# A decode layer on one core: TensorE's program as a loop of four turns, K and V loaded head by head, the maximum gathered by TensorE, w1 loaded behind wq

## The chip, the core and the metric

One core of a Trainium2 chip runs the kernel. The metric is device time in microseconds (us) of one execution; the kernel before takes 111.0 us (median of 3 runs, 110.99 to 111.12). Its engines: TensorE (PE; PEld is its weight load), VectorE (DVE), ScalarE (ACT), GpSimd (POOL), and SyncE (SP), whose queue issues the large loads. 16 DMA engines carry all loads.

## The reference

```python
xn = layernorm(x)                                          # x: 2 x 1 x 448
q  = xn @ wq                                               # 16 heads of 256
k, v = the last 2048 positions of the caches, 8 heads, each used by 2 heads of q
s  = softmax(q k / 16) v @ wo                              # 4096 -> 448
g  = silu(relu(xn @ w1) @ w2)                              # 448 -> 1792 -> 448
return x + s * g
```

All inputs are bf16. Of the 44 MB that are read, K and V are 33.5 MB (2 batches x 8 heads x 2048 x 256, twice), wq and wo 3.67 MB each, w1 and w2 1.61 MB each.

## The kernel before, in words

**Units.** The attention is done in four units `u`: one batch and four of the eight K/V heads, 4 MiB of K and 4 MiB of V each. A unit's position is split into 32 blocks `kb` of 64 positions `t`. `load_k` and `load_v` (lines 279, 282) move a unit with one DMA each; `unit_src` (line 197) puts block kb of head h on partition 4 kb + h, so that the four heads are interleaved over all 128 partitions, one row of 32 KiB on each.

**A unit's steps.** `do_T` (line 312): DVE transposes 32x32 blocks of K (pairs of bf16 as one fp32) from `kbuf` to `kt`, in four pieces. `do_S` (line 318): 32 matmuls in four column groups of TensorE make the scores, 8 rows in each quarter of the partitions; the moving operand takes every eighth bf16 of `kt` (step of 16 bytes). `ch_max` (line 330): DVE takes each row's maximum and shares it over the heads' rows by two 32x32 transposes and a second maximum; ACT's exponential follows. `ch_spread` (line 344): 16 matmuls lay the exponentials out by position, and one more sums them. `ch_pt` (line 355): DVE copies this with a mask. `do_PV` (line 363): 32 matmuls, in four column groups, with contiguous rows of V. `do_o_pe`, `do_at_exp`, `do_at` (lines 375 to 401): the unit's output is turned and scaled into `at2`.

**The second branch.** `do_h`, `do_hn`, `do_hT`, `do_hs` (lines 408 to 433) and `do_F` (line 450) are the two layers with w1 and w2.

**The end.** `at2` meets wo's 32 row groups j (lines 531 to 544). wo comes in five DMAs (`WO_PARTS`). The first 24 groups run in four column groups (`tiled`, line 435), each 448 columns wide, whose partial sums `fold_sums` (line 440) copies and adds; the last 8 groups run as four narrow matmuls each, straight into the result.

**What sets the order.** Each engine runs its instructions in the order in which lines 202 to 551 append them to `_Prog.lists`; a wait on a semaphore is put before an instruction that needs another engine's result. The order is written out by hand: unit u+1's scores stand between unit u's steps, with two buffers each for K, `kt`, the scores, the exponentials and `pt`. SP's order is wq, K0, K1, V0, K2, K3, V1, V2, w1, V3, w2, and wo's five parts. V2 goes to a K buffer (`vhome`, line 211), w1 and w2 to `kt[0]` after unit 2's scores.

Of the kernel before, what the change touches and what calls it, by code (L numbers as in the profile page):

```python
# [5 lines left out]
BF = mybir.dt.bfloat16  # L6
# [9 lines left out]
class _Op:  # L16
    __slots__ = ("eng", "fn", "deps", "dma", "needed", "value", "sem")

    def __init__(self, eng, fn, deps, dma):
        self.eng, self.fn, self.deps, self.dma = eng, fn, deps, dma  # L20
        self.needed, self.value, self.sem = dma, 0, None


class _Prog:


    def __init__(self, nc, es):
        self.nc, self.es = nc, es
        self.lists = {PE: [], DVE: [], ACTE: [], SP: [], POOL: []}

    def op(self, eng, fn, deps=()):
        o = _Op(eng, fn, [d for d in deps if d is not None], False)
        self.lists[eng].append(o)
        return o

    def dma(self, eng, dst, src, deps=()):
        o = _Op(eng, lambda e: e.dma_start(dst, src), [d for d in deps if d is not None], True)
        self.lists[eng].append(o)
        return o

    def run(self):
# [3 lines left out]
        for ops in self.lists.values():  # L45
            for o in ops:
                for d in o.deps:
                    d.needed = True
        for e, ops in self.lists.items():
            sem, count = self.es.enter_context(self.nc.semaphore(f"s_{e}")), 0  # L50
            for o in ops:
                if o.dma:
                    n += 1
                    o.sem, o.value = self.es.enter_context(self.nc.semaphore(f"d_{n}")), 16
                elif o.needed:
                    count += 1
                    o.sem, o.value = sem, count
        engines = ((POOL, nc.gpsimd), (SP, nc.sync), (ACTE, nc.scalar), (PE, nc.tensor), (DVE, nc.vector))
        for name, eng in engines:
            hint = eng.mark_branch_hint_location() if name == DVE else None  # L60
            self.emit(eng, self.lists[name])
            if hint is not None:
                eng.br("fin").branch_hint(hint)
        nc.switch_bb("fin")

    def emit(self, eng, ops):
        seen = {}
        for o in ops:
# [9 lines left out]
            if o.needed:  # L78
                made.then_inc(o.sem, 16 if o.dma else 1)


def bass_recurrent_scan__sliding_block_cached__dense_activation_relu__decode_kernel(
# [30 lines left out]
    WO_PARTS = [10, 10, 4, 6, 2]  # L113
    WO_TILED = 24

    es = contextlib.ExitStack()
    with es:
# [21 lines left out]
        hmask = named("hmask", [128, 4], F32)  # L139
# [9 lines left out]
        q_big = named("q_big", [128, NU * NG * 32], BF)  # L149
# [7 lines left out]
        mx = named("mx", [128, 32], F32)  # L157
        mxt = named("mxt", [128, 32], F32)
        nbt = named("nbt", [128, 32], F32)
        nb = [named(f"nb{i}", [128, 32], F32) for i in range(2)]  # L160
        ssum = [named(f"ssum{i}", [128, 1], F32) for i in range(2)]
        rs = [named(f"rs{i}", [128, 1], F32) for i in range(NU)]
        e_sb = [named(f"e_sb{i}", [128, 512], BF) for i in range(2)]
        pt = [named(f"pt{i}", [128, 512], BF) for i in range(2)]
        fs = named("fs", [128, D], F32)
        o_sb = named("o_sb", [128, 512], BF)
        at_exp = named("at_exp", [128, 64], BF)
# [3 lines left out]
        kt = [named(f"kt{i}", [128, UW], BF) for i in range(2)]  # L171
        wq_sb = kt[1]
        wo_sb = kbuf[1]
        w1_sb = kt[0]
        W2_AT = SLOTS * FC

        sp = psum("sp", [128, 2048], F32)
        sbk = [sp[:, 512 * i:512 * i + 512] for i in range(2)]
# [18 lines left out]
        def unit_src(u, cache):  # L197
            hf, b = divmod(u, 2)
            return cache[b, HU * hf:HU * hf + HU, SK - W:SK, :].rearrange("h (kb t) d -> kb h (t d)", t=TS)
# [11 lines left out]
        vhome = [vbuf, vbuf, kbuf[0], vbuf]  # L211
        d_k, d_v = {}, {}
# [7 lines left out]
        p_qb = pr.op(POOL, lambda e: e.memset(q_big[:, :].bitcast(F32), 0.0))  # L220
        p_s0 = pr.op(POOL, lambda e: e.memset(sel[:, :].bitcast(F32), 0.0))
        p_mx = pr.op(POOL, lambda e: e.memset(mx[:, :], 0.0))
        p_nbt = pr.op(POOL, lambda e: e.memset(nbt[:, :], 0.0))
# [3 lines left out]
        a_z = [pr.op(ACTE, lambda e, t=t: e.memzero(t[:, :])) for t in (mbk, gbk, hbk)]  # L227
# [21 lines left out]
        def fold_op(e):  # L249
# [3 lines left out]
        v_hm = pr.op(DVE, lambda e: e.tensor_reduce(  # L253
            out=hmask[:, :], in_=view(ident, 0, [[1, 4], [4, 32]]), axis=AX.X, op=ALU.add), [p_id])

        def fold8_op(e):
            with nc.allow_low_precision("zeros and ones"):
                return e.tensor_reduce(out=fold8[:, :], in_=view(ident, 0, [[32, 4], [4, 2], [1, 4]]), axis=AX.X, op=ALU.add)
        v_f8 = pr.op(DVE, fold8_op, [p_id])
        v_ss = pr.op(DVE, lambda e: e.tensor_copy(  # L260
            view(sumsel, 0, [[64, 2], [8, 8], [1, 8]]), view(fold8, 0, [[0, 2], [1, 8], [0, 8]])), [v_f8])
        v_ff = pr.op(DVE, lambda e: e.tensor_copy(fold_f[:, :], fold[:, 0:17]), [v_fold])
        for r in range(2):
            v_sel = pr.op(DVE, lambda e, r=r: e.tensor_copy(
                view(sel, 1024 * r, [[132, 8], [32, 4], [1, 4]]), view(ident, 4 * r, [[0, 8], [1, 4], [32, 4]])), [p_s0, p_id])
# [7 lines left out]
        for r in range(1, 4):  # L273
            v_xr = pr.op(DVE, lambda e, r=r: e.tensor_copy(
                view(xr, 32 * r, [[128, SLOTS], [1, 4]]), view(xr, 0, [[128, SLOTS], [1, 4]])), [v_xr])
# [3 lines left out]
        def load_k(u, deps=()):  # L279
            d_k[u] = pr.dma(SP, kbuf[u % 2][:, :], unit_src(u, A_k_cache), deps)  # L280

        def load_v(u, deps=()):
            d_v[u] = pr.dma(SP, vhome[u][:, :], unit_src(u, A_v_cache), deps)


        def do_q():
# [19 lines left out]
            for qd in range(4):  # L306
                st["q"] = pr.op(DVE, lambda e, qd=qd: e.tensor_copy(  # L307
                    view(q_big, qd, [[NG * 32, NU], [32, NG], [4, 8]], n=32, p0=32 * qd),
                    view(q_t, 0, [[1, NU], [32, NG], [256, 8]], n=32, p0=32 * qd)), [v, p_qb])


        def do_T(u, c):
            src, dst = kbuf[u % 2][:, :].bitcast(F32), kt[u % 2][:, :].bitcast(F32)
            deps = [d_k[u], st.get(("S", u - 2))] + ([st["q_mm"]] if u == 1 else [])
            st["T", u] = pr.op(DVE, lambda e: e.transpose(  # L315
                dst[:, 2048 * c:2048 * c + 2048], src[:, 2048 * c:2048 * c + 2048]), deps)

        def do_S(u):
            deps = [st["T", u], st["q"], st.get(("exp", u - 2)), *st["q_n"]]
            for gp in range(NG):  # L320
                for h in range(HU):
                    lo = (u * NG + gp) * 32 + 8 * h
                    o = pr.op(PE, mm(sbk[u % 2][32 * h:32 * h + 8, :], q_big[:, lo:lo + 8],
                                     view(kt[u % 2], 64 * (gp // 2) + gp % 2 + 2 * h, [[256, TS], [8, 8]]),
                                     gp == 0, gp == NG - 1, tile_position=(0, 32 * h)), deps)
                    deps = []
            st["S", u] = o


        def ch_max(u):  # L330
            k = u % 2
            v = pr.op(DVE, lambda e: e.tensor_reduce(out=mx[:, 0:1], in_=sbk[k], axis=AX.X, op=ALU.max),  # L332
                      [st["S", u], p_mx, st.get("mxt")])
            v = st["mxt"] = pr.op(DVE, lambda e: e.transpose(mxt[:, :], mx[:, :]), [v, st.get("neg")])  # L334
            v = st["neg"] = pr.op(DVE, lambda e: e.tensor_reduce(
                out=view(nbt, 0, [[4, 2], [1, 4]]), in_=view(mxt, 0, [[4, 2], [0, 4], [1, 4]]),
# [244 lines left out]
```

## Time and profile before

| | |
|---|---|
| median of 3 runs | 111.0 us |
| the profiled execution | 111.33 us |
| its span, first to last instruction | 109.9 us |
| moved by the DMA engines | 44.16 MB, mean 402 GB/s |
| PE, DVE, ACT busy | 68.5, 59.8, 12.2 us |
| instructions | 1131 (490 matmuls, 469 weight loads) |

The profiled execution is 0.33 us over the median, and 1.4 us of it lie outside the span. Busy time is a mean over stages with different limits; a matmul's length is modelled, and matmuls in different column groups overlap, so the time from the first to the last of a group says more than the sum of their lengths.

### The profile page before, as it was taken

The page shows a single profiled execution, that of the slowest core. Times are in us where ns is not written, and L with a number is a line of the kernel's source. Part 1 is how long each engine was busy: PE and PEld are TensorE (multiplying, and loading weights), DVE is VectorE, ACT ScalarE, POOL GpSimd, SP SyncE. Part 2 cuts the span into 40 slices and gives each one's busy share as a digit, 9 for nine tenths or more (in the row PEclk, how much of TensorE's full clock was granted, in tenths as well). Part 3 has the DMA queues.
Part 4 walks back from the last instruction along what each step waited for, and adds up shares of the span by engine and source line. Part 5 has one row for each costly group of instructions (what it writes and reads, how often), then busy time and mean ns, then how long its engine had stood idle before and what let it go on. Part 6 is the DMA issues. An engine that isn't in the chain of part 4 may idle for free.

```text
span 109.9 us, 1131 instructions
## 1 busy us (share of the span) xinstructions
PE 68.5 (62%) x490; PEld 23.3 (21%) x469; DVE 59.8 (54%) x84; ACT 12.2 (11%) x21; POOL 4.4 (4%) x14
## 2 busy tenths in 40 slices
PE   0010699500001995579995699989999892556871
PEld 0000001000000110553110622146213841211330
DVE  2167000399999996825984879995005026003621
ACT  2930000340000000201000200040001300020000
POOL 7800000000000000000000000000000000000000
PEclk9999999995555599656999755999999999955555
DMA  6798998999899989989999999999899998999920
GB/s 168 334 460 388 513 430 382 418 489 430 382 501 441 394 382 525 430 382 406 483 430 394 430 489 406 394 477 447 344 425 496 453 406 363 413 433 417 413 115 1
DMA packets 2463, 44.16 MB, mean 402 GB/s; under 512 B 282, under 2 KB 412, under 8 KB 924
## 3 DMA queue, kind: packets, MB, share of 16 engines
q1 hardware_dynamic: 2432, 44.11, 94.3%
q8 instruction: 3, 0.05, 0.2%
q10 hardware_dynamic: 28, 0.01, 0.0%
HBM read 44.11 MB, written 0.00 MB: 402 GB/s over the span
## 4 chain that ended last, share of the span: by engine, by line
DMA 36%; PE 32%; DVE 26%; issue 2%; ACT 1%; SPq 0%
DMA kbuf<-in_A_wo_dram 26%; PE sp L187 23%; DVE kt L315 15%; DMA kt<-in_A_wq_dram 10%; PE sp L192 6%; DVE q_t L305 2%; DVE mx L332 2%; DVE q_big L307 2%; PE gbk L187 2%; ACT e_sb L339 1%; PE hbk L187 1%; DVE q_n L299 1%; DVE pt L356 1%; DVE mxt L334 1%; DVE nb L338 1%
## 5 line engine op out<-in xcount | busy, mean ns | idle before, releaser
L187 PE MATMUL sp<-kt,q_big 128*8 128x512 bf16 x128 | 30.1, 1088 | 14.4 <-DVE kt L315 14.4
L315 DVE STREAM_TRANSPOSE kt<-kbuf 128x2048 f32<-128x2048 f32 x16 | 35.6, 2274 | 2.8 <-DMA kbuf<-in_A_k_cache_dram 2.7
L187 PEld LDWEIGHTS sp<-kt,q_big 128*8 128x8 bf16 x128 | 4.7, 103 | 34.0 <-issue 18.4
L187 PE MATMUL sp<-e_sb,sel 128*128 128x64 bf16 x64 | 8.1, 294 | 5.3 <-ACT e_sb L339 5.3
L187 PE MATMUL sp<-vbuf,pt 128*16 128x512 bf16 x96 | 8.0, 492 | 2.4 <-DMA vbuf<-in_A_v_cache_dram 1.9
L187 PEld LDWEIGHTS sp<-e_sb,sel 128*128 128x128 bf16 x64 | 7.0, 119 | 8.2 <-ACT e_sb L339 8.2
L339 ACT ACTIVATE e_sb<-sp,nb 128x512 bf16<-128x512 f32 x4 | 2.8, 688 | 51.5 <-DVE nb L338 51.5
L332 DVE TENSOR_REDUCE mx<-sp 128x1 f32<-128x512 f32 x4 | 2.7, 687 | 9.4 <-PE sp L187 9.4
L192 PE MATMUL sp<-kt,xr 128*128 128x512 bf16 x21 | 7.7, 488 | 0.0
L299 DVE TENSOR_SCALAR q_n<-sp 128x1024 bf16<-128x1024 f32 x1 | 1.2, 1225 | 10.5 <-PE sp L192 10.5
L187 PE MATMUL sp<-kt,xr 128*128 128x512 bf16 x7 | 3.6, 512 | 3.7 <-DMA kt<-in_A_wq_dram 3.7
L187 PE MATMUL mbk<-ident,xg 2*128 2x2 bf16 x7 | 0.3, 163 | 7.9 <-DVE xg L237 7.9
L356 DVE TENSOR_TENSOR pt<-sp,hmask 128x512 bf16<-128x512 f32 x4 | 2.8, 698 | 4.2 <-PE sp L187 4.2
L387 DVE TENSOR_TENSOR at_exp<-mbk,qmask 128x64 bf16<-128x64 f32 x4 | 0.8, 204 | 7.2 <-PE mbk L187 7.2
L187 PEld LDWEIGHTS sp<-vbuf,pt 128*16 128x16 bf16 x96 | 3.1, 120 | 7.0 <-DMA vbuf<-in_A_v_cache_dram 3.7
L372 ACT ACTIVATE o_sb<-sp 128x512 bf16<-128x512 f32 x4 | 2.4, 593 | 17.9 <-PE sp L187 17.9
L399 DVE TENSOR_SCALAR at<-mbk,rs 64x32 bf16<-64x32 f32 x4 | 1.4, 350 | 3.6 <-PE mbk L187 3.6
L187 PEld LDWEIGHTS sp<-kt,xr 128*128 128x128 bf16 x7 | 0.8, 121 | 10.7 <-issue 6.9
L187 PE MATMUL gbk<-kbuf,at 128*17 128x448 bf16 x24 | 3.0, 570 | 0.1
L302 ACT ACTIVATE q_n<-sp 128x1024 bf16<-128x1024 f32 x1 | 1.0, 1024 | 14.5 <-PE sp L192 14.5
L187 PE MATMUL gbk<-kt,h_sb 128*17 128x448 bf16 x14 | 1.7, 569 | 1.3 <-DMA kt<-in_B_w_dram 1.3
L305 DVE STREAM_TRANSPOSE q_t<-q_n 128x2048 bf16<-128x2048 bf16 x1 | 2.3, 2311 | 0.0
(74 smaller groups left out, 45.8 us busy)
## 6 DMA issues: line engine op xcount, KB each, us to landing
kbuf<-in_A_k_cache_dram SPq DMA_DIRECT2D x4, 4096.0 KB, 17.9
vbuf<-in_A_v_cache_dram SPq DMA_DIRECT2D x3, 4096.0 KB, 21.6
kbuf<-in_A_v_cache_dram SPq DMA_DIRECT2D x1, 4096.0 KB, 18.7
kt<-in_A_wq_dram SPq DMA_DIRECT2D x1, 3584.0 KB, 11.2
kt<-in_B_w_dram SPq DMA_DIRECT2D x2, 1568.0 KB, 19.3
kbuf<-in_A_wo_dram SPq DMA_DIRECT2D x2, 1120.0 KB, 27.3
kbuf<-in_A_wo_dram SPq DMA_DIRECT2D x1, 672.0 KB, 29.3
kbuf<-in_A_wo_dram SPq DMA_DIRECT2D x1, 448.0 KB, 29.1
```

What stands on the lines that cost most here:

```text
L187: return lambda e: e.matmul(out_ap, lhsT=lhsT, rhs=rhs, start=start, stop=stop, skip_group_check=True, **kw)
L192: return lambda e: e.add_instruction(mybir.InstMatmult(name=nc.get_next_instruction_name(), start_tensor_calc=start, stop_tensor_calc=stop ...
L299: e.tensor_scalar(out=view(q_n, 0, [[64, 16], [32, 2], [1, 32]]), in0=view(sp, 0, [[64, 16], [1, 2], [2, 32]]), scalar1=SCALE, scalar2=Non ...
L305: v = pr.op(DVE, lambda e: e.transpose(q_t[:, :], q_n[:, :]), halves)
L307: st["q"] = pr.op(DVE, lambda e, qd=qd: e.tensor_copy(view(q_big, qd, [[NG * 32, NU], [32, NG], [4, 8]], n=32, p0=32 * qd), view(q_t, 0, [ ...
L315: st["T", u] = pr.op(DVE, lambda e: e.transpose(dst[:, 2048 * c:2048 * c + 2048], src[:, 2048 * c:2048 * c + 2048]), deps)
L332: v = pr.op(DVE, lambda e: e.tensor_reduce(out=mx[:, 0:1], in_=sbk[k], axis=AX.X, op=ALU.max), [st["S", u], p_mx, st.get("mxt")])
L334: v = st["mxt"] = pr.op(DVE, lambda e: e.transpose(mxt[:, :], mx[:, :]), [v, st.get("neg")])
L339: st["exp", u] = pr.op(ACTE, lambda e: e.activation(e_sb[k][:, :], sbk[k], ACT.Exp, bias=nb[k][:, 0:1], accum_out=ssum[k][:, 0:1]), [v, st ...
L356: st["pt", u] = pr.op(DVE, lambda e: e.tensor_tensor(out=view(pt[u % 2], 0, [[128, 4], [1, 128]]), in0=view(sp, 1024, [[0, 4], [1, 128]]), ...
L372: st["osb", u] = pr.op(ACTE, lambda e: e.activation(o_sb[:, :], obk[:, :], ACT.Copy), [o, st.get(("oT", u - 1))])
L399: st["at", u] = st["mbk"] = pr.op(DVE, lambda e: e.tensor_scalar(out=view(at2, 16 * b, [[32, 32]], n=64, p0=p0), in0=mbk[p0:p0 + 64, 32:64 ...
```

## The change

- **TensorE's program is a loop.** After wq's and w1's matmuls, a loop `pe_loop` of four turns does one unit a turn, one step after the other, with waits against a register that counts the turns. A block for w2 is entered in the fourth turn alone. `kt`, the scores, the exponentials, `pt` and V have one buffer each.
- **K and V.** A load moves one head: head h goes to partitions 32 h to 32 h + 31, one row of 32 KiB on each. A unit's K takes four DMAs instead of one, and so does its V; V of units 2 and 3 comes in halves of positions, eight DMAs, the first half as soon as the first 16 matmuls of the unit before have read it.
- **Scores.** With this layout a column group of TensorE takes eight blocks kb of all four heads, and the moving operand takes every second bf16 (step of 4 bytes). A unit's q is laid out by four small ACT copies in each turn instead of by DVE once.
- **Maximum.** A multiply on DVE and a matmul with a matrix of zeros and ones replace the two transposes.
- **w1** is loaded to V's buffer right behind wq, and its layer is done ahead of the loop, on ACT instead of DVE. w2 goes to the buffer that held wq.
- **wo** comes in parts of 10, 12, 6, 2, 2 groups instead of 10, 10, 4, 6, 2, and 28 groups instead of 24 run in column groups.
- SP's order is wq, w1, K0, K1, V0, K2, V1, K3, V2 (halves), w2, V3 (halves), wo.

The diff, cut to its core:

```diff
-    WO_PARTS = [10, 10, 4, 6, 2]
-    WO_TILED = 24
+    WO_PARTS = [10, 12, 6, 2, 2]
+    WO_TILED = 28
...
-        def unit_src(u, cache):
+        def cache_src(u, cache, h):
             hf, b = divmod(u, 2)
-            return cache[b, HU * hf:HU * hf + HU, SK - W:SK, :].rearrange("h (kb t) d -> kb h (t d)", t=TS)
+            return cache[b, HU * hf + h, SK - W:SK, :].rearrange("(kb t) d -> kb (t d)", t=TS)
...
         def load_k(u, deps=()):
-            d_k[u] = pr.dma(SP, kbuf[u % 2][:, :], unit_src(u, A_k_cache), deps)
+            d_k[u] = [pr.dma(SP, kbuf[u % 2][32 * h:32 * h + 32, :], cache_src(u, A_k_cache, h), deps) for h in range(HU)]
...
+        def load_v_half(u, k):
+            lo, hi = k * UW // 2, (k + 1) * UW // 2
+            for h in range(HU):
+                pr.dma(SP, vbuf[32 * h:32 * h + 32, lo:hi], cache_src(u, A_v_cache, h)[:, lo:hi],
+                       [st["PV" if k else "PVa", u - 1]], kind="VB" if k else "VA")
...
         def ch_max(u):
-            v = st["mxt"] = pr.op(DVE, lambda e: e.transpose(mxt[:, :], mx[:, :]), [v, st.get("neg")])
...
+            st["mxd"] = pr.op(DVE, lambda e: e.tensor_scalar(
+                out=mxd[:, :], in0=qmask[:, :], scalar1=mx[:, 0:1], scalar2=None, op0=ALU.mult),
+                [v, v_qm, st.get(("max", u - 1))], kind="MX")
...
+            pe.br("turn")
+            with block("turn"):
+                wait("QB", r)
+                wait("T", r)
+                for gp in range(NG):
+                    for s in range(4):
+                        o = mm(sbk[32 * s:32 * s + 8, :], qb[:, 8 * gp:8 * gp + 8],
+                               view(kt, 64 * (gp // 2) + gp % 2 + 16 * s, [[256, TS], [2, 8]]),
+                               gp == 0, gp == NG - 1, tile_position=(0, 32 * s))(pe)
+                o.then_inc(pr.kinds["S"], 1)
+                wait("MX", r)
+                mm(xbk[:, 4:8], same[:, :], mxd[:, :], True, True)(pe).then_inc(pr.kinds["max"], 1)
+                pe.br_lt(r, NU, on_true="spread", on_false="second_layer")
+            with block("second_layer"):
+                do_F(pe)
+                pe.br("spread")
+            with block("spread"):
+                hint = pe.mark_branch_hint_location()
+                wait("EXP", r)
...
+                wait("PT", r)
+                for k in range(2):
+                    wait("VB" if k else "VA", v64)
...
+                pe.br_lt(r, NU + 1, on_true="turn", on_false="tail").branch_hint(hint)
...
+        d_w1 = pr.dma(SP, w1_sb[:, 0:SLOTS * FC], w1_src)
         load_k(0)
         load_k(1)
         do_q()
+        do_h()
...
+        load_v(0, [st["h", 0], st["h", 1]])
         load_k(2, [st["T", 0]])
...
+        for u in range(NU):
+            ch_max(u)
+            ch_exp(u)
+            if u < NU - 1:
+                do_qb(u + 1)
+                do_T(u + 1, 0)
+            else:
+                copy_sums(st["F"])
+            ch_pt(u)
+            if u < NU - 1:
+                for c in range(1, 4):
+                    do_T(u + 1, c)
+            do_osb(u)
+            do_at_exp(u)
+            do_at(u)
+            if u == 0:
+                load_v(1)
+                load_k(3, [st["T", 1]])
+        load_v_half(2, 0)
+        load_v_half(2, 1)
+        pr.dma(SP, w2_sb[:, 0:14 * D].rearrange("p (hf f) -> p hf f", hf=2), w2_src, [st["q_mm"]], kind="w2")
+        load_v_half(3, 0)
+        load_v_half(3, 1)
```

## The prediction, made before the changed kernel was run

> **What bounds the kernel now.** I read three views in this order: the DMA rows of the page, the table of stages, and the timeline of the end.
>
> The page's DMA row gives in 40 slices the tenths in which the 16 DMA engines were busy; the row below it gives what they moved, and the third what of it was program code.
>
> ```profile
> DMA  6798998999899989989999999999899998999920
> ...
> DMA packets 2463, 44.16 MB, mean 402 GB/s; under 512 B 282, under 2 KB 412, under 8 KB 924
> ...
> q8 instruction: 3, 0.05, 0.2%
> ```
>
> The engines are full from the fourth slice to the last but two. The stages (start and end, length, busy time and count of PE, PEld, DVE, ACT, POOL, granted clock, DMA share, GB/s) say the same with numbers:
>
> ```profile
> 51.00:63.00 12.00, 9.87 (x60) 3.14 (x53) 9.95 (x9) 1.38 (x3) 0.00 (x0) 0.93 1.00 430
> 63.00:75.00 12.00, 11.48 (x83) 4.19 (x81) 10.96 (x11) 1.27 (x3) 0.00 (x0) 0.77 1.01 437
> 75.00:87.00 12.00, 11.65 (x89) 4.28 (x88) 2.42 (x8) 1.27 (x3) 0.00 (x0) 1.00 1.02 436
> ```
>
> PE too is busy, but the DMA share is 1.00 at 430 to 437 GB/s whatever PE and DVE do: 4 MiB of K or V take 9.7 us. The end shows that the stream sets the time (start, length, instruction, and in brackets the idle time before it and its cause):
>
> ```profile
> 102.35 3.12 PE L187 MATMUL gbk<-kbuf,at 128*17 128x448 bf16 x24
> ...
> 103.79 0.12 PEld L187 LDWEIGHTS gbk<-kbuf,at 128*17 128x17 bf16 x8 [0.92 <-DMA kbuf<-in_A_wo_dram]
> ...
> 104.88 0.10 PEld L187 LDWEIGHTS gbk<-kbuf,at 128*17 128x17 bf16 x4 [0.60 <-DMA kbuf<-in_A_wo_dram]
> 105.50 0.62 DVE L442 COPY fs<-gbk 128x448 f32<-128x448 f32 x1 [1.15 <-PE gbk L187]
> ...
> 106.50 0.75 PEld L187 LDWEIGHTS hbk<-kbuf,at 128*17 128x17 bf16 x32 [0.17 <-DMA kbuf<-in_A_wo_dram]
> 106.53 0.97 PE L187 MATMUL hbk<-kbuf,at 128*17 128x112 bf16 x32
> ```
>
> PE waits for each part of wo. So nothing is won by a faster engine; what counts is how fast the stream runs, whether it pauses, and what follows its end.
>
> **The stream: same bytes, no fetch.** In the trace's DMA records each DMA engine reports the end of its share of a load. K2's 16 reports lie between 50.03 and 50.62 us, 0.6 apart; those of wo's last part between 104.97 and 107.01, 2.0 apart. In between three packets of code, 16 KB each, ran at 52.3, 75.8 and 91.3 us for 0.96, 0.95 and 0.89 us, and the 32 KB packet behind each took 1.7 us instead of 1.21. A load has landed when its slowest engine reports, so the fetches cost 2.0 - 0.6 = 1.4 us at the end. PE had begun some 240 matmuls and weight loads at the first fetch, and between 200 and 270 more lay between the fetches. The new program has about 410 written out instead of 959. Bounds for what is won: 1.4 us (no fetch) and nothing (as many fetches); below nothing if each turn fetches its blocks anew (second rival). I take 1.4, since half of the program ran before the first fetch here.
>
> K and V come in 40 DMAs instead of 8. Each closes with a packet of 9 ns on every engine: 32 x 9 ns = +0.3 us. Heads and rows otherwise keep their 32 KB (halves: 16 KB) packets; I take the rate of the rows above. Issuing costs SP 0.54 us each, 2.2 us for four: V3's second half waits for PV of unit 2 (done at about 84.7), while V3's first half and w2 keep the queue full to 92. So wo's last part lands at 107.0 - 1.4 + 0.3 = 105.9 us.
>
> **A turn against the stream.** All steps of a unit now stand in a row, and DVE's transposes for the next unit begin only when this unit's scores are read. By rows of before: scores S; maximum 0.72 (row sum with its gap); multiply 0.20 (like the 0.19 and 0.20 us rows of this size); matmul of the maximum 0.5 (the fp32 sum `xbk`: 0.49); second maximum 0.2; exponential 0.84 and spread 2.07, beside one transpose piece; `pt` and reciprocal 0.8; three pieces 6.7; `at_exp` and its matmul 0.5: 12.5 us + S. The two transposes that go saved 0.46, so the new maximum costs 0.3 more; the turn hides it.
>
> S is the open size. These two rows are the same number of matmuls with the same columns, one with a step of 16 bytes, one on contiguous rows:
>
> ```profile
> 75.70 7.51 PE L187 MATMUL sp<-kt,q_big 128*8 128x512 bf16 x32
> ...
> 83.28 1.93 PE L187 MATMUL sp<-kbuf,pt 128*16 128x512 bf16 x32
> ```
>
> The first takes 7.5 us also at 35.3, where the clock was half for a time, so not the clock but the reading binds it. The new step is 4 bytes: S lies between 1.93 (3.62 at the lower clock, 48.0 us) and 7.51, and I take 1.9 to 3.6 as nearest to the contiguous rows. [...]
>
> A turn is then 14.4 to 16.1 us, against 19.4 us in which the next unit's K and V land. Followed through, with wq at 11.9, w1 15.6, K0 25.3, K1 35.0, V0 44.7, K2 54.4, V1 64.1, K3 73.8, V2 78.7 and 83.5, w2 87.2, V3 92.1 and 96.9: the turns' steps wait for K2, V1, K3, V2, V3, never the reverse, and each buffer is free 6 us or more before the queue runs dry. K0 comes 3.7 us later behind w1, but transposes start at 25.4, before 26.35 as now, because q's four copies (1.8 us) leave DVE. These, 0.2 to 0.44 us each on ACT, lie beside DVE's 6.7 us; the first four stand behind w1's layer on ACT, which ends by about 30, under unit 0's transposes (to 34.3). Branches and register steps are not in the trace: from nothing to 1 us (a fetch's length) each; 3 to 5 us of slack a turn hide both. If that cover were gone, each would count in full.
>
> **The end.** V3 lands at 97.2; PV's half 1.9, copy 0.6, turn 0.3, 0.25, matmul 0.25, scale 0.4: `at2` at 100.9. 22 wide matmuls in rounds of four at 0.42 (14 for w2 took 1.67) need 2.3 us, so PE is ready for the third part at 103.9 after the first fold. 28 groups have landed two parts (0.53 us each) before the end: 104.8, where 24 had landed at 104.84. Six wide matmuls, two rounds: 0.60 + 0.42; copy 0.66; fold 0.04 + 0.35; 16 narrow ones at 30 ns (32 in 0.97): 0.50. The last ends at 107.35 instead of 107.52; what follows is unchanged. So the larger `tiled` part gives most of the fetch's gain back.
>
> **Sum**: -1.4 + 0.3 + 0.9 in the tail = -0.2 us of the profiled execution's 111.33; that stands 0.33 above the median, so **110.8 us** on the median's scale. About 0.2% is what a measurement of this kernel can tell from no change, 0.2 us: the forecast lies on that edge. Its own range is 110.0 (full clock for the tail's matmuls, about -0.5, and a little more of the fetches' tail) to 111.6 (half of the fetches back).
>
> **Rivals.**
>
> *The stream halves (39%, slower).* Before, the 16 engines write rows spread over all 128 partitions at once. Now each load lies on 32, and all 16 engines work on the same quarter at the same time; the ends 0.6 us apart show how closely they march. If two engines then share one way into these partitions, a 32 KB packet takes 2.43 us instead of 1.21 and each of the eight K and V loads 19.4 instead of 9.7: +77.6, 188.4 us. Being 0.6 us out of step saves that twice a load, 10 us: 179. I take 184, within 176 to 189. It decides from the first percent: the queue has no slack, 1% on K and V is 0.8 us and more than the gain. For it: 430 GB/s is the same in all windows, so a fixed limit is being met; against it: nothing in the trace says that this limit sits at the partitions and not in the engines, whose packets all run at 27 GB/s. [...]
>
> *Code is still fetched (8%, slower).* The loop jumps back over block borders; if it costs as much as the three fetches, the tail's 0.9 and 0.3 remain: +1.2, 112.0. The page's 0.2% for code would stay or grow.
>
> *The scores stay slow (6%, slower).* With S at 7.5 a turn is 20 us and longer than the stream's 19.4; unit 3's scores end at 102.3, its output at about 113, the last matmul at 117.4: 121 us.
>
> **How the numbers follow.** Forecast 47%: faster 25%, no change 12%, slower 10%. With the rivals: faster 25%, no change 12%, slower 63%. Range: to leave out no more than 2 in 10 it must reach into the halved stream, so 109.9 to 189; the forecast's own is 110.0 to 111.6.
>
> **What would show it.** Right: no or one packet of code, DMA share 1.00 at 430 GB/s in every stage to 95 us, the 32 score matmuls in 2 to 4 us, the transposes waiting for K2 and K3, last wide matmuls waiting for wo's third part at 104.8. Wrong: a DMA share of 1.00 at about 215 GB/s (the engines wait inside their packets), transposes waiting 10 us or more for K; or a DMA share below 0.9 between 50 and 95 us, with V's loads waiting for PE.

## The result and the profile after

The changed kernel takes 195.12 us (median of 4 runs, 193.79 to 196.17), the kernel before 111.06 on the same chip (4 runs, 110.99 to 111.16): a ratio of 1.756, 95% interval 1.745 to 1.767. The profiled execution took 195.08 us, its span 192.7. The forecast of 110.8 was wrong, and the time lies 6 us above the range's end of 189: the rival of the halved stream came in, and larger than it was priced. Where a kernel was run several times, the medians and ratios below are of its fast executions; three of the ten of loop_whole_timed, over 1.5% above its fastest, are left out (with them its median is 112.65).

The page's DMA rows (tenths of 40 slices in which the engines were busy, what they moved, and the queue that carries program code):

```profile
DMA  7999999999999999999999999997999999999990
GB/s 256 411 415 237 211 218 218 218 218 218 204 218 204 218 184 204 190 218 211 218 218 218 218 211 211 204 218 160 214 214 214 208 349 222 211 218 210 351 394 11
...
q8 instruction: 1, 0.02, 0.0%
```

The first row looks like the one before: the engines are busy from the second slice to the last but one. The second tells the difference. While wq and w1 come (slices 2 and 3) they move 411 to 415 GB/s, with K's first head 237 and then 160 to 222, but for one slice of 349 where w2 comes, and at the end, with wo, 351 to 394 again. A busy row says that the engines have packets, not that the packets move: 160 to 222 GB/s here. The table of stages shows the same (start and end, length, busy time and count of PE, PEld, DVE, ACT, POOL, granted clock, DMA share, GB/s):

```profile
5.00:15.00 10.00, 3.32 (x15) 0.53 (x10) 3.97 (x17) 1.39 (x2) 0.00 (x0) 1.00 1.10 438
...
56.00:96.00 40.00, 8.68 (x89) 4.78 (x89) 11.28 (x11) 2.21 (x7) 0.00 (x0) 0.59 1.01 210
```

In the trace's DMA records a packet of 32 KB of K or V took 2.57 us (median), 1.21 in the kernel before, while wq's packets of 28 KB took 1.06 as before. The page's groups show who waited (busy us, mean ns; idle time before, and what ended it):

```profile
L349 DVE STREAM_TRANSPOSE kt<-kbuf 128x2048 f32<-128x2048 f32 x16 | 35.8, 2283 | 38.9 <-DMA kbuf<-in_A_k_cache_dram 38.9
L220 PE MATMUL sp<-vbuf,pt 128*16 128x512 bf16 x128 | 14.8, 627 | 84.4 <-DMA vbuf<-in_A_v_cache_dram 84.4
```

The difference of the two profiled executions, 195.08 - 111.33 = 83.75 us, is made up so: the last part of wo lands at 188.87 instead of 107.01 (+81.86); the last narrow matmul ends 1.51 us behind it instead of 0.49 (+1.02); from there to the span's end it is 2.4 in both; and 2.3 us lie outside the span instead of 1.5 (+0.9).

The rest went nearly as foretold. The scores, the maximum's matmuls and the end in the timeline (start, length, instruction, in brackets the idle time before):

```profile
45.73 3.58 PE L220 MATMUL sp<-kt,qb 128*8 128x512 bf16 x32 [21.49 <-DVE kt L349]
...
82.25 1.90 PE L220 MATMUL sp<-kt,qb 128*8 128x512 bf16 x32 [0.35 <-issue]
85.21 0.38 PE L220 MATMUL xbk<-mxd,same 128*128 128x4 f32 x2 [1.06 <-DVE mxd L363]
...
187.78 0.92 PE L220 MATMUL gbk<-kbuf,at 128*17 128x448 bf16 x6 [0.37 <-DMA kbuf<-in_A_wo_dram]
```

The 32 score matmuls take 1.90 us at a granted clock of 1.00 and 3.58 at 0.50, instead of 7.51. The wide matmuls of the end wait for wo's third part. But none of this could shorten a run whose loads take twice as long.

### The profile page after: what moved, and what is told of

It reads as the page before. It is cut to its first block, busy times and chain, and to the rows that moved or that the text cites. A ratio compares the mean times of both kernels' runs of the same rounds, so it can differ in the third digit from the quotient of the medians.

```text
span 192.7 us, 1208 instructions
## 1 busy us (share of the span) xinstructions
PE 57.3 (30%) x486; PEld 23.6 (12%) x458; DVE 56.8 (29%) x73; ACT 16.9 (9%) x40; POOL 4.0 (2%) x13
## 4 chain that ended last, share of the span: by engine, by line
DMA 67%; another core or an unknown queue 12%; PE 8%; DVE 6%; SPq 5%; issue 1%; ACT 0%; DVEq 0%
DMA vbuf<-in_A_v_cache_dram 36%; DMA kbuf<-in_A_k_cache_dram 17%; DMA kbuf<-in_A_wo_dram 14%; PE sp L220 7%; DVE kt L349 5%; SPq L52 5%; PE hbk L220 1%; PE gbk L220 0%; PE xbk L220 0%; ACT e_sb L370 0%; DVE mx L362 0%; DVE fs L487 0%; DVE tmp L575 0%; DVE out_sb L577 0%
## 5 line engine op out<-in xcount | busy, mean ns | idle before, releaser
L220 PE MATMUL sp<-vbuf,pt 128*16 128x512 bf16 x128 | 14.8, 627 | 84.4 <-DMA vbuf<-in_A_v_cache_dram 84.4
L220 PE MATMUL sp<-kt,qb 128*8 128x512 bf16 x128 | 12.1, 543 | 22.4 <-DVE kt L349 21.5
L220 PEld LDWEIGHTS sp<-vbuf,pt 128*16 128x16 bf16 x128 | 4.5, 130 | 91.4 <-issue 73.9
L383 ACT ACTIVATE o_sb<-sp 128x512 bf16<-128x512 f32 x4 | 2.4, 597 | 106.4 <-PE sp L220 106.4
L225 PE MATMUL sp<-wf,xr 128*128 128x512 bf16 x21 | 7.1, 457 | 0.0
L220 PEld LDWEIGHTS sp<-kt,qb 128*8 128x8 bf16 x128 | 3.6, 107 | 28.5 <-issue 27.8
L220 PE MATMUL sp<-wf,xr 128*128 128x512 bf16 x7 | 3.4, 484 | 3.7 <-DMA wf<-in_A_wq_dram 3.7
L355 ACT ACTIVATE qb<-q_t 32x16 bf16<-32x16 bf16 x16 | 3.7, 234 | 0.1
L375 DVE TENSOR_TENSOR pt<-sp,qmask 128x512 bf16<-128x512 f32 x4 | 2.6, 662 | 1.6 <-PE sp L220 1.6
L220 PE MATMUL xbk<-mxd,same 128*128 128x4 f32 x8 | 1.7, 288 | 4.2 <-DVE mxd L363 4.2
L220 PE MATMUL gbk<-vbuf,xr 128*128 128x448 bf16 x7 | 2.5, 353 | 0.0
L225 PE MATMUL hbk<-vbuf,xr 128*128 128x448 bf16 x7 | 2.5, 352 | 0.0
```

What stands on the lines that cost most here:

```text
L220: return lambda e: e.matmul(out_ap, lhsT=lhsT, rhs=rhs, start=start, stop=stop, skip_group_check=True, **kw)
L225: return lambda e: e.add_instruction(mybir.InstMatmult(name=nc.get_next_instruction_name(), start_tensor_calc=start, stop_tensor_calc=stop ...
L355: st["qb", u] = pr.op(ACTE, lambda e, qd=qd: e.activation(view(qb, qd, [[8, NG], [4, 2]], n=32, p0=32 * qd), view(q_t, u + 512 * qd, [[32, ...
L375: st["pt", u] = pr.op(DVE, lambda e: e.tensor_tensor(out=view(pt, 0, [[256, 2], [64, 4], [1, 64]]), in0=view(sp, 1024, [[64, 2], [0, 4], [ ...
L383: st["osb", u] = pr.op(ACTE, lambda e: e.activation(o_sb[:, :], obk[:, :], ACT.Copy), [st["PV", u], st.get(("oT", u - 1))], kind="OSB")
```

## The experiments

Two theories for the stream stood at the start. **Places**: a load to 32 neighbouring partitions is slow because of where they lie. **Count**: 40 loads of at most 1 MiB with 32 rows each are slower than 8 of 4 MiB, wherever they go. A third question was what the loop is worth with loads at full rate. Times without an interval are of a single execution; beside them the kernel before took 110.8 to 111.6.

### The loads, in the kernel before and after

**loop_whole_loads**: the changed kernel with the loads of before.

```diff
-            d_k[u] = [pr.dma(SP, kbuf[u % 2][32 * h:32 * h + 32, :], cache_src(u, A_k_cache, h), deps) for h in range(HU)]
+            d_k[u] = [pr.dma(SP, kbuf[u % 2][:, :], unit_src(u, A_k_cache), deps)]
```

> The changed kernel with K and V loaded as before (one DMA per unit, heads interleaved over 128 partitions; V of units 2 and 3 in two halves). Rows of K and V then lie on other partitions than the loop takes them to, so the output is not the reference's; the instructions of the engines are unchanged. Theory (the 32-partition loads alone cost the time): 9.7 us per 4 MiB, 430 GB/s, 110 to 112 us. Rival (the loop's waits hold the loads back): stays above 150 us.

112.94 us, packets of 1.21 us, 9.7 us for 4 MiB. (In this kernel and in the others of the loop with whole loads, the heads lie interleaved while the scores are made for one head in each quarter, so that queries meet keys of other heads; kind and number of all operations are the same.) The page:

```profile
DMA  6798999999999999999989999999999999999910
...
DMA packets 2748, 44.11 MB, mean 400 GB/s; under 512 B 314, under 2 KB 572, under 8 KB 956
```

There is no row for the code queue any more. So 82 of the 84 us are the way K and V are loaded, and the loop on its own is still not faster: that is taken up below.

**before_quarter_loads**: the kernel before, with nothing but the loads of after.

```diff
-            d_k[u] = pr.dma(SP, kbuf[u % 2][:, :], unit_src(u, A_k_cache), deps)
+            d_k[u] = [pr.dma(SP, kbuf[u % 2][32 * h:32 * h + 32, :], <head h, rows kb>, deps) for h in range(HU)]
```

> The kernel before with four DMAs for each unit's K and V, head h on partitions 32 h to 32 h + 31, and nothing else changed; the heads then lie on other partitions than the scores take them from, so the output is not the reference's. Theory (32 neighbouring partitions halve the stream): 32 KB packets of 2.4 to 2.6 us, 4 MiB in 20 us, 188 to 196 us. Rival (more DMAs, not their partitions, or the loop): 111 to 114 us.

194.25 us; packets of 2.56 us from the very first of K. (Here, and in before_quarter_lagged, the steps read K and V as if they lay as before, so that heads and positions are mixed; the other kernels with moved loads keep each row where the steps look for it.) The change of loads alone makes the whole loss.

**before_strided_loads**: as many loads of as many rows, from the same places in memory, but head h goes to partitions h, h + 4, h + 8 and so on.

```diff
+            d_k[u] = [pr.dma(SP, view(kbuf[u % 2], 0, [[1, UW]], n=32, p0=h, pstep=4), <head h, rows kb>, deps) for h in range(HU)]
```

> The kernel before with four DMAs for each unit's K and V, one per head, but head h on partitions h, h + 4, h + 8 and so on: the same 32 rows and the same count of DMAs as in the changed kernel, spread over all 128 partitions, and each block on the partition that it has before. If what counts is that a load lies in one quarter of the partitions: 111 to 113 us. [...] If the number of DMAs counts: about 190 too, but then the stream in halves of 64 partitions is near 111.

111.13 us, packets of 1.21 us. The stages of the two, 20 us each, quarter loads first:

```profile
40.00:60.00 20.00, 7.48 (x32) 1.07 (x32) 8.84 (x6) 0.00 (x0) 0.00 (x0) 0.67 1.01 210
```
```profile
40.00:60.00 20.00, 16.34 (x102) 5.45 (x94) 13.94 (x13) 1.38 (x3) 0.00 (x0) 0.83 1.03 440
```

Count is out: 24 loads more than in the kernel before cost nothing that can be seen, and source, size and number are the same in both. Only the place written to differs.

**before_half_loads**: two loads of 64 neighbouring partitions for each unit.

```diff
+            d_k[u] = [pr.dma(SP, kbuf[u % 2][4 * lo:4 * hi, :], unit_src(u, A_k_cache)[lo:hi], deps) for lo, hi in ((0, 16), (16, 32))]
```

> The kernel before with two DMAs for each unit of K and of V, one for partitions 0 to 63 and one for 64 to 127; the layout, the bytes and all else as before. 16 blocks lie outermost in each, so that all 16 DMA engines take part. If 64 neighbouring partitions share ways as 32 do: packets of 32 KB take about 2.56 us, and the time is 188 to 196. If only 32 rows are too few and 64 are enough: packets of 1.21 us and 111 us. If it is in between (a way for each 32 partitions): packets of 1.8 us, 150 us.

193.69 us, 2.56 us a packet. 64 neighbours of one half are no better than 32: 211 GB/s between 60 and 100 us, 210 in before_quarter_loads, against 424 to 440 in before_strided_loads.

**before_middle_loads**: partitions 32 to 95 in one load, then 0 to 31 and 96 to 127 (`for lo, hi in ((8, 24), (0, 8), (24, 32))`). The author's estimate, from the 9.7 and the 20.0 us that 4 MiB took: if the middle load runs at the full rate and the outer two at half, a unit of K or V takes 4.9 + 2 x 5.0 us, and the whole 150 to 154 us.

> The kernel before with three DMAs for each unit's K and V, each block on the partition that it has before: first partitions 32 to 95 (64 of them), then 0 to 31, then 96 to 127. [...] Rival (only the number of partitions counts, 64 at half or three quarters of the rate): 4 MiB in 20 us, 188 to 196 us, or, if 64 neighbours are enough and 32 not, still about 150 with the middle load's packets longer than 1.3 us.

169.09 us, neither. The first middle load, over both halves, moved 2 MiB in 4.85 us, the full rate: all 64 of its packets took 1.21 us, where those of the first load of before_half_loads, with as many neighbouring partitions and the same listing, took 1.8 to 2.6. So 64 neighbours are slow from 0 to 63 (211 GB/s in before_half_loads) and fast from 32 to 95. But the outer loads, with 8 blocks outermost, show 8 reports in the records instead of 16: read as 8 engines carrying them. Two causes are mixed in these, and the whole time decides nothing.

**after_two_queues** and **after_heads_crossed**: the changed kernel, the first with heads 2 and 3 (`h > 1`) issued from ACT's queue, the second with the heads in the order 0, 2, 1, 3.

```diff
-    pr.dma(SP, kbuf[u % 2][32 * h:32 * h + 32, :], ...
+    pr.dma(ACTE if h > 1 else SP, kbuf[u % 2][32 * h:32 * h + 32, :], ...
```

> The changed kernel, with the loads of heads 2 and 3 (partitions 64 to 127) issued from ACT's queue and those of heads 0 and 1 from SP's as before; layout, sizes and waits are the same. Theory: the halved rate comes from all 16 engines writing into the same half of the partitions at once. If an engine that has work in two queues moves both at once, its packets go to both halves and the rate comes back: DMA rows of 400 GB/s and more from 5 to 95 us, and 112 to 116 us in all. If the engines take turns between the queues packet by packet and stay in step, all are still in one half at any time: 2.56 us a packet, 193 to 196 us. In between (some pairs out of step): 130 to 180.

> The changed kernel with the heads of each load in the order 0, 2, 1, 3, so that every load follows one in the other half of the partitions. By the theory that a half is shared by all, only packets that cross the change of halves are quicker (2.30 instead of 2.56 us in before_quarter_loads): now every change of load is such a crossing, three more in each eight loads; 0.26 us less at most at each, 40 loads: 186 to 193 us. If each quarter had a way of its own and no more, nothing changes: 194 to 196.

194.03 and 190.87 us. Two queues, one for each half, do not bring the rate back: 223 GB/s between 60 and 100 us. Either it is not enough to feed both halves, or the engines stay in step through two queues as through one; neither is shown. Crossed heads gain 4 us, as foretold: packets at a change of halves take 2.34 us, the others 2.57.

**before_quarter_lagged** was to put the engines out of step: one useless load ahead, whose 8 outer blocks were to go to 8 engines alone (8 reports in before_middle_loads).

```diff
+        d_lag = pr.dma(SP, vbuf[0:128:4, :], <32 rows of K, 8 blocks outermost>)
         d_wq = pr.dma(SP, wq_sb[:, 0:SLOTS * HC], wq_src)
```

> before_quarter_loads (one DMA for each head, to 32 neighbouring partitions; 194.25 us) with one load more at the very start: 1 MiB whose 8 outer blocks go to 8 of the 16 DMA engines, 128 KB each, over partitions spread by fours; its data are not used. From then on these 8 engines are four packets of 32 KB, two heads, behind the other 8: while one group writes heads 2 and 3 (the upper half) the other writes heads 0 and 1 (the lower). Theory of the step: the halves are then always shared by 8 engines each, packets fall to 1.21 us, DMA rows read 400 GB/s and more, the reports of a load spread over 4.9 us, and the time is 111.1 + 4.9 = 116, up to 122. If the pairs that share a way lie inside a group, or if a load of 32 partitions is slow for a reason of its own: packets stay at 2.56 us, 196 to 199. If only some pairs are split: between.

232.84 us, far above all that was expected. The lag was there (a load's reports spread over 9.4 us, about four packets), and yet the packets of K took 2.56 us: from 56 to 96 us the engines moved 209 GB/s. The rest of the time over 194 comes from the lag itself, which four packets of the useless load made 14 us long, and from stages in which packets took 3.4 to 3.9 us. The theory of halves alone, in which 8 engines in each half would have been at full rate, falls. What was left was the second outcome: engines that share a way were in the same group, which no record shows, or such a load is slow for a reason of its own.

**before_strided_regrouped** asks whether the partitions that a load covers decide alone. They are those of before_strided_loads, which ran at 424 to 440 GB/s; only the rows of a load are listed as 16 times 2 instead of 32.

```diff
-                "(kb t) d -> kb (t d)", t=TS), deps) for h in range(HU)]
+                "(kr kq t) d -> kq kr (t d)", kr=2, t=TS), deps) for h in range(HU)]
```

> before_strided_loads (one DMA for each head, to every fourth partition; 1.21 us a packet, 111.13 us) with the blocks of each load taken in another order: 16 outer times 2 inner blocks instead of 32, so that the loads still cover the same partitions with the same rows, but the 32 rows may be dealt to the 16 engines in another way (positions lie in other places, for K and V alike; the attention is over the same positions). [...] If only the partitions that a load covers count, as in the theory of the halves: 1.21 us, 111.

181.93 us. The author had put 180 to 194 us for the case that two engines then meet at one way in, which no record shows. A packet took 2.30 us; the stage from 60 to 100 us:

```profile
60.00:100.00 40.00, 16.73 (x109) 6.65 (x111) 12.11 (x15) 1.38 (x3) 0.00 (x0) 0.63 0.99 225
```

Same partitions, same bytes, same number of loads, and half the rate: 225 GB/s against 424 to 440. That the partition written to decides was shown above (210 against 424 to 440 GB/s); this says that covering good partitions is not enough, and that how a load's rows are listed counts too. (The order in which the source is read changes with the listing, so this run alone does not rule out the source.) Why it counts is not shown. The author takes it that the listing decides which partitions the engines write to *at the same time*; but the records name neither the engine of a packet nor the partition that it writes to, so this is inferred, not seen.

### The loop, with loads at full rate

**loop_whole_timed** is loop_whole_loads, timed in 10 executions, **straight_whole_loads** is the same with the four turns written out (`for r in range(1, NU + 1):` instead of the blocks and branches), and **loop_small_parts** has wo in the parts of before.

```diff
-    WO_PARTS = [10, 12, 6, 2, 2]
-    WO_TILED = 28
+    WO_PARTS = [10, 10, 4, 6, 2]
+    WO_TILED = 24
```

> The changed kernel with K and V in whole units over all 128 partitions, as in one look before, now timed against the kernel before. The look gave 112.94 beside 110.82. If the 2.1 us are real: 112.7 to 113.2, slower by 1.5 to 2.1%. If they were chance, as the forecast would have it: 110.8, no difference. Terms expected from the look: the stream ends about 0.65 us earlier than in the kernel before, the last narrow matmul 0.4 later, and 2.6 us instead of 1.4 lie outside the span.

> The kernel of loop_whole_timed with TensorE's four turns written out one behind the other, without a branch; the order of every engine's work is the same. Theory: the loop keeps code fetches out of the span and pays for it with one behind its end. Then two or three packets of 16 KB of code appear in the span, the 16 reports of wo's last part spread from 0.9 to about 2 us, the stream ends 1 to 1.4 us later than with the loop, and what lies outside the span falls from 2.6 to about 1.4 us: in sum 112.8 to 113.4, no better than the loop. Rival: the time outside the span has nothing to do with the loop; then it stays at 2.6 and the sum is 114.0 to 114.4. Second rival: fetches don't hold up the stream; then the stream ends where it does with the loop, and the time is 111.8.

> The kernel of loop_whole_timed with wo in parts of 10, 10, 4, 6, 2 groups and 24 in column groups, as before the change. Theory: the larger third part holds up the fold. With 24 groups landed at about 104.2 (the stream ends 0.65 earlier than in the kernel before, where they landed at 104.84), the fold is done before the last part lands and the last narrow matmul ends 0.5 us behind the stream's end, at about 106.9 instead of 107.9: 0.6 to 1.0 us less than loop_whole_timed, 112.0 to 112.3, still slower than the kernel before for what lies outside the span. Rival: the parts make no difference, 112.9.

| kernel | median us | to before, 95% | stream ends | 16 KB code packets in the span | outside the span |
|---|---|---|---|---|---|
| loop_whole_timed | 112.40 | 1.005 to 1.014 | 106.2 (106.4 in loop_whole_loads) | 0 | 2.3 to 2.7 in six of ten, 3.3 to 3.7 in four |
| straight_whole_loads | 113.53 | 1.017 to 1.033 | 107.1 | 3 | 2.3 to 3.3 |
| loop_small_parts | 112.82 | 1.011 to 1.021 | 106.2 | 1 | 2.3 to 2.4 |

Half of the first theory held: without the loop three code packets come back, the reports of wo's last part spread over 1.6 us instead of 0.7, and the stream ends 0.9 later. The other half failed: the time outside the span stayed. So the loop is not its cause. (The profiled execution of loop_whole_timed is one of the four with the longest end; a 16 KB code packet ran 2.4 us behind its span. The other three were not profiled.)

loop_small_parts came out 0.5 us above its forecast, and its timeline shows why:

```profile
105.31 0.39 PE L220 MATMUL hbk<-fs,fold_f 128*17 128x112 f32 x8 [0.72 <-DVE fs L485]
105.69 0.79 PE L220 MATMUL hbk<-kbuf,at 128*17 128x112 bf16 x31
107.83 0.22 PE L220 MATMUL hbk<-kbuf,at 128*17 128x112 bf16 x1 [1.35 <-issue]
```

The fold was done in time, and 31 of 32 narrow matmuls ran with the last part, but the last one waited 1.35 us for nothing that the profile names. A 16 KB code packet ran at 105.39 for 1.08 us. With 12 matmuls more in the tail, TensorE's program had run past what was fetched, as it seems. loop_middle_parts below, with 24 narrow matmuls instead of 32, bears this out: it has such a packet too, at 105.35, and there it is the branch closing TensorE's program that takes 1.53 us, where it takes 0.20 in loop_whole_timed. Behind the last matmul that holds nothing up.

**before_more_on_act** and **loop_less_on_act** test a new theory for the time outside the span. In the DMA records, every profiled execution with the long end has a code packet of 8 KB 1.4 to 1.5 us behind the last instruction, and ACT has 53 instructions in them instead of 27. The first adds instructions to the kernel before, the second takes them from the loop.

```diff
+            for i in range(26):
+                pr.op(ACTE, lambda e, i=i: e.activation(spare[0:2, i:i + 1], sd[0:2, 0:1], ACT.Copy), ...)
```
```diff
-                st["qb", u] = pr.op(ACTE, lambda e, qd=qd: e.activation(
+                st["qb", u] = pr.op(DVE, lambda e, qd=qd: e.tensor_copy(
```

> The kernel before with 26 copies of two numbers on ACT between 22 and 44 us, where ACT waits for the first maximum; nothing reads them. Theory: the 1.0 us more outside the span, which the changed kernel and the loop with whole loads have, is a fetch of 8 KB of program code behind the last instruction, and it is there because ACT has 53 instructions instead of 27 and its program no longer ends in what was fetched at the start. Then a packet of 8 KB appears about 1.5 us behind the span's end, 2.4 to 2.6 us lie outside the span instead of 1.4, and the time is 112.0 to 112.3, 1.0% slower. Rival: it comes from the blocks and branches of the new program; then there is no such packet and the time is 111.1.

> The kernel of loop_whole_timed with q's 16 small copies on DVE instead of ACT. By the same theory ACT's program is short enough again: no packet of code behind the span's end, 1.4 to 1.6 us outside the span, and 111.5 to 111.8 us instead of 112.65. By the rival (blocks and branches): still 2.4 us and more outside the span, 112.5 to 112.9. The copies take DVE about 0.5 us a turn, which the turn's slack hides. As in loop_whole_timed, K and V lie in other partitions than the scores are made for, so that each head meets positions of the other heads; the work is the same in kind and number.

Before_more_on_act: 112.63 us, ratio 1.010 (1.007 to 1.014). The profiled span is 109.8, no longer than before's, and the 26 copies are done long before the first maximum:

```profile
21.09 2.51 ACT L306 ACTIVATE spare<-sd 2x1 f32<-2x1 f32 x26
```

The 8 KB packet is there at 111.22, and 2.3 to 2.6 us lie outside the span. Loop_less_on_act, with 37 instructions on ACT: no such packet in the profiled execution, 1.4 to 1.6 us outside the span in 8 of 10 runs, 111.31 us, ratio 1.0004 (0.9965 to 1.0044). The theory holds from both sides: with 26 idle instructions that touch nothing, 0.8 us more lie outside the span (medians of 2.4 against 1.6 in the kernel before beside them). The medians of the whole differ by 1.3; the other 0.4 or so lie within the span (110.2 against 109.8), and no run says why. after_two_queues fits too: with 73 instructions on ACT the 8 KB packet ran inside the span, at 165.35, and 1.4 us lay outside.

**loop_middle_parts**: loop_less_on_act with `WO_PARTS = [10, 10, 6, 4, 2]` and `WO_TILED = 26`.

> loop_less_on_act (111.31) with wo in parts of 10, 10, 6, 4, 2 groups and 26 in column groups. The last narrow matmul ended 1.14 us behind the stream's end there, 0.5 in the kernel before. Theory: the third part, landed at 105.3, is late; with 26 groups it lands 0.5 to 0.6 us earlier, and the last matmul ends 0.5 to 0.7 behind the stream: 110.7 to 111.0. Rival: more narrow matmuls push TensorE's code over the border again, as in loop_small_parts, where the last of 32 waited 1.35 us: then a gap before the last matmuls, and 111.8 to 112.2. K and V lie for other heads than the scores are made for, as in loop_whole_loads.

110.57 us beside 111.55, ratio 0.992 (0.989 to 0.994). The end:

```profile
104.52 0.92 PE L220 MATMUL gbk<-kbuf,at 128*17 128x448 bf16 x6 [0.35 <-DMA kbuf<-in_A_wo_dram]
...
106.16 0.58 PE L220 MATMUL hbk<-fs,fold_f 128*17 128x112 f32 x8 [0.72 <-DVE fs L485]
...
106.51 0.79 PE L220 MATMUL hbk<-kbuf,at 128*17 128x112 bf16 x24
```

The last narrow matmul ends at 107.30, 1.13 us behind the stream's end at 106.17, with no gap before it. That is as far behind as in loop_less_on_act (1.14), not the 0.5 to 0.7 foretold: the 0.3 us by which it ends earlier are those by which the stream itself ended earlier. The medians differ by 0.7. But this execution, with a span of 109.6, is one of three long ones; in the other seven the span is 108.8 to 109.3, and none of them was profiled, so where the gain comes from is not settled. This is the fastest of all, with the heads mixed as said above; with heads where the kernel before has them and loads at full rate, the scores would read with the old step of 16 bytes and take 7.5 us a turn.

### The scores' step

**before_scores_pairs**: the kernel before, with two blocks of one head next to each other, so that the scores read pairs 4 bytes apart.

```diff
-                view(kt[u % 2], 64 * (gp // 2) + gp % 2 + 2 * h, [[256, TS], [8, 8]])
+                view(kt[u % 2], 64 * (gp // 2) + gp % 2 + 4 * h, [[256, TS], [16, 4], [2, 2]])
```

> The kernel before with K's blocks laid out so that two blocks of the same head are neighbours (block 2 kq + r of head h on partition 8 kq + 2 h + r, K in two DMAs of 64 partitions spread by twos); the scores read the same numbers in pairs 4 bytes apart, one pair in every 16 or 32 bytes, and the rest is as before. The 32 matmuls took 7.51 us with one bf16 used of 16 bytes, and 1.9 with four. If a line of 16 bytes is fetched once and two hits in it are enough: 1.9 us. If the time goes by the hits, up to four: 3.8. If a step over 4 bytes is what counts: 7.5. The whole stays at 111 in any case, since the loads set the end, and the loads of 64 spread partitions run at 1.21 us a packet.

The scores take 3.8 to 3.9 us. Two neighbouring rows at a granted clock of 1.00, the scores and the contiguous rows of V:

```profile
118.58 3.91 PE L187 MATMUL sp<-kt,q_big 128*8 128x512 bf16 x32
...
122.55 1.93 PE L187 MATMUL sp<-kbuf,pt 128*16 128x512 bf16 x32
```

So 7.51, 3.91 and 1.90 us for one, two and four numbers used of each 16-byte piece touched: in these rows the time goes by the number of pieces, down to the 1.9 that contiguous rows take as well. Two numbers in a piece are not enough for the 1.90 us of four. The total was a surprise: 153.27 us instead of 111. K's loads, to every second partition with 16 outer rows of four heads, ran at half rate (mostly 2.3 to 2.6 us a packet), V's, as before, at 1.21. It was the first hint that spread partitions are not enough, and led to before_strided_regrouped.

## Why the prediction was wrong

**The step that failed** is "Heads and rows otherwise keep their 32 KB (halves: 16 KB) packets; I take the rate of the rows above". The rate of the rows above, 9.7 us for 4 MiB, was a property of loads over 128 partitions, and no row of before showed another kind. On 32 neighbouring partitions 4 MiB take 20.0 us, and the kernel before with these loads alone takes 194.25. Kept or not, it decided over 80 us; the rival that said so was given 39% against 47%. "Nothing in the trace says that this limit sits at the partitions and not in the engines" was true of the trace, and was read as evidence for the engines. It was none: all of K's and V's loads in that trace lie over 128 partitions, at a median of 1.21 us a packet, and such rows can't tell the two limits apart. The two runs that differ in the place alone do: 210 GB/s in before_quarter_loads, 424 to 440 in before_strided_loads.

**The rival's size.** Its sum is built on two engines that share one way into the partitions. No run shows that term; what the runs show in its place is the rate, 210 GB/s on 32 neighbours against 424 to 440 on every fourth partition, and packets of 2.57 us (after) and 2.56 (before_quarter_loads) against 1.21. Its 184 us were 11 too low. The saving from being out of step, of which the 184 hold 4.4 us, did not come. A unit's loads of K or V take 20.0 us (a head lands 4.85 and 5.15 us behind the last in turn) and not the 19.4 of a mere doubling, 4.8 us on eight units of K and V. The 0.9 us outside the span were in neither its 184 nor its range; the tail's 0.9 was, through the 110.8 that it starts from. About 1 us of the 11 is left and not taken apart here. Three quarters of the 32 KB packets take 2.57 us and a quarter about 2.3, 2.51 in the mean, not twice 1.21 = 2.43; why it is more than a doubling is open.

**What hit.** The code: one 16 KB packet in the span, behind the last matmul, instead of three. With loads at full rate that was worth 0.6 to 0.8 us at the stream's end, not 1.4, since the engines are 0.7 to 0.9 apart without fetches too (loop_whole_timed, loop_whole_loads). The counts behind that term were read roughly: 227 matmuls and weight loads had begun at the first fetch, and 280 and 192 lay between the fetches. More loads cost nothing that can be seen (24 more in before_strided_loads), where 0.3 was put for 32. The scores, 1.90 and 3.58 us (1.9 to 3.6 foretold). The maximum: multiply 0.23, matmul 0.38 to 0.58, second maximum 0.16 (0.20, 0.5, 0.2 foretold). The turn hid all of it, as foretold, also at full rate, where the loops' streams end no later than that of the kernel before. The tail: last narrow matmul 1.5 us behind the stream's end, foretold 1.45.

**What was not foretold**: 0.8 to 0.9 us outside the span. "What follows is unchanged" looked at the instructions; with 26 more on ACT a packet of 8 KB of code ran at 194.17 us, 1.4 us behind the last instruction. So even at full rate the change as made would have cost 0.9% (112.40), not won 0.2%: -0.7 at the stream's end, +1.0 in the tail, +0.8 outside the span, worked out from the rows above.

## What to carry to other kernels

A rate read off a trace holds for the shape of the transfers it was read from (here 430 GB/s over 128 partitions, 210 on 32 neighbours): before a layout is changed, ask which partitions each load writes to and how its rows are listed, and try the new shape alone, in the old kernel, first. When loads set the time, keep to a listing of rows and partitions that was seen to run at full rate. Spreading the rows alone is not enough: before_strided_regrouped spread them by fours, as before_strided_loads did, and ran at 225 GB/s instead of 424 to 440. And look at the ends: 26 instructions more on an idle ACT came with 0.8 us more outside the span.

## What the runs showed of the hardware

- 32 rows on every fourth partition: 424 to 440 GB/s; on 32 neighbours 210, on 64 in one half 211; on every fourth, but listed as 16 times 2: 225. 64 neighbours over both halves (32 to 95): packets of 1.21 us, the full rate.
- In before_middle_loads the loads with 8 outer blocks show 8 reports instead of 16.
- A code packet of 16 KB took 0.9 to 1.1 us with loads at full rate, and the reports of the loads behind it lie further apart (0.6 us before the first and 2.0 after the third in the kernel before); three of them, with the turns written out, came with a stream's end 0.9 us later. In loop_small_parts one came late and TensorE stood for 1.35 us, in loop_middle_parts its closing branch for 1.53; that packet and stop belong together is inferred.
- ACT with 53 instead of 27 instructions: an 8 KB code packet behind the end, and 0.8 us more outside the span. With 37 there was none in the profiled execution, and 2 of 10 executions had the long end all the same, as had 3 of 19 of the kernel before beside them; why is open.
- The records of taken branches in the loop (after, loop_whole_timed) are 0.20 to 0.23 us long, those of branches not taken 0.07; in loop_whole_timed the stream ends at 106.2 all the same, 107.0 in the kernel before.
